# Pooled attention with a mixture-of-depths block: the first pair's queries copied by thirds, its keys all turned before the first scores

## The chip, the cores and the metric

The kernel runs on one core of a Trainium2 chip. A core has five engines that run their own instruction streams and wait for each other through semaphores: TensorE (matrix products and transposes; in the profile PE, its weight loads PEld), VectorE (DVE), ScalarE (ACT), GpSimd (POOL) and SyncE (SP), which here issues most transfers. The metric is the device time of one execution in microseconds. The kernel before takes 711.04 us, the median of three runs (710.81 to 711.89). Its profiled execution has a span of 707.8 us from the first to the last instruction, and all times inside a profile are counted from the start of that span.

## The reference

Two blocks follow one another. The first is attention whose queries are pooled by two along the sequence; the second routes 128 tokens of each batch entry through a small feed-forward network.

```python
# q, k, v: (8, 8, 1152, 64) float32
q_pool = q.reshape(B, H, S // 2, 2, D).mean(axis=3)          # 576 queries
scores = (1 / np.sqrt(D)) * np.matmul(q_pool, k.transpose(0, 1, 3, 2))
attn = np.exp(scores - scores.max(-1, keepdims=True))
attn = attn / (attn.sum(-1, keepdims=True) + 1e-09)
x = np.matmul(attn, v)                                       # then (B, 576, 512)
...
s = np.einsum('bsd,d->bs', x, w_gate)                        # a score per token
# the 128 best tokens of each batch entry b:
ye = np.maximum(xe @ w1, 0.0) @ w2                           # 512 -> 1024 -> 512
out[b, top_idx] = x[b, top_idx] + sigmoid(s)[:, None] * ye   # others: out = x
```

## The kernel before

Everything that the timed run does lies in the class `_Plain`; the other function in the file is a fallback for scores outside a numeric range. The work is cut into 32 **pairs** (8 batch entries times 4 pairs of heads), each pair into two **halves** of 288 of the 576 pooled queries. Keys and queries must stand with the head dimension on the partitions, "turned", before TensorE can multiply them: two heads of 64 fill the 128 partitions. `kT` holds the turned keys of a pair (128 x 1152), `qT` its turned and pooled queries (128 x 576).

For each half there are nine **blocks**, each of 128 keys (`scores`, L807). A block is four small products (quarter arrays, recorded as eight matmuls at L818) into one of four PSUM buffers, each two banks wide (`banks`, L996), and one exponential on ScalarE (L825) that moves the block to SBUF and so frees the buffer. GpSimd and VectorE sum the exponentials (`folded`, L859 and L864). The weighted sum with the values (`weighted`, L838) comes one half later. The order of all instructions on every engine is written out by hand in `run` (L1300): scores of half 0, scores of half 1, weighted sum of half 0, scores of half 2, weighted sum of half 1, and so on, with pieces of the routed feed-forward block (L1205, L1218) strewn in between. TensorE works through its instructions in that order. The framework adds the semaphore waits; it follows regions of a tile, so that a matmul waits only for the writers of the columns which it reads.

From the second pair on, keys and queries come in an order that lets VectorE turn them (L735, L739), in `prepare_pair`. **The first pair is special**, because nothing runs beside it. `load_first` (L741) fetches it in few, large pieces: queries on ScalarE's queue (L755), keys on SyncE's in four transfers (L759), first three of the nine chunks of both heads, then six of both; then the values (L762). `prepare_first` (L765) adds neighbouring queries (L776), and has TensorE turn keys (L783, in `keys`, L780) and queries (L794) against an identity matrix into PSUM. The results are copied to `kT` (L788) and `qT` (L801). The keys come in two steps: chunks 0 to 2 are turned first and copied by ScalarE; chunks 3 to 8 are turned later, by a function that `prepare_first` gives back. `run` hands it to the first call of `scores` as `behind_first`, where it is called once the first block and its exponential have been issued. VectorE copies that second part.

The six query transposes fill two PSUM banks, three transposes of 96 columns in each. A copy out of PSUM also has to sort columns: by their number's remainder by three (t in the code) they go into three thirds of `qT`, of 192 columns each. Before, VectorE copies bank 0 and ScalarE bank 1; each writes 96 columns in every third.

Ten products of ones (L612) run ahead of all this, while the data are on the way. `constants` (L616) follows `prepare_first` on VectorE and GpSimd: it makes tables that are used much later (slot numbers at L633, token numbers at L637, and so on).

Of the kernel before, what the change touches and what calls it, by code (L numbers as in the profile page):

```python
# [10 lines left out]
P = 128  # L11
BLK = 32

G = 3
# [13 lines left out]
def _any_scores(  # L28
# [451 lines left out]
    in_pair = [(j, t) for j in range(2) for t in range(NF)] + [(0, NF)]  # L480
    upcoming = load_pair(*pairs[0])
    run(prepare_pair(upcoming))
    preparing = iter(())
    routing = iter(())
# [50 lines left out]
class _Plain:  # L535
# [229 lines left out]
    def prepare_first(self, pair):  # L765

        nc, NC, D = self.nc, self.NC, self.D
        kT = pair["kT"] = self.load.tile([P, self.S], F32, name="kT")
        qT = pair["qT"] = self.load.tile([P, self.Sp], F32, name="qT")
        rows, third = 3 * BLK, self.QB // 3  # L770
        acc = self.work.tile([P, G, 2 * self.HALF], F32, name="acc")
        qp = acc.rearrange("p u n -> p (u n)")[0:rows, 0 : 2 * third * D]
        qp = qp.rearrange("p (n j d) -> p n j d", j=2, d=D)
        of = pair["q"].rearrange("p j (n r) d -> p n j r d", r=2)
        for j in range(2):
            nc.vector.tensor_tensor(  # L776
                out=qp[:, :, j, :], in0=of[:, :, j, 0, :], in1=of[:, :, j, 1, :], op=ALU.add
            )

        def keys(a, z, copy):  # L780
            ps = self.banks().rearrange("p b n -> p (b n)")
            for c in range(a, z):
                nc.tensor.transpose(  # L783
                    ps[:, (c - a) * P : (c - a + 1) * P],
                    pair["k"][:, c, :, :].rearrange("p j d -> p (j d)"),
                    self.ident[:, :],
                )
            copy(kT[:, a * P : z * P], ps[:, 0 : (z - a) * P])  # L788

        keys(0, G, nc.scalar.copy)  # L790
        ps = self.banks()
        per = third // 2
        for n in range(third):
            nc.tensor.transpose(  # L794
                ps[:, n // per, n % per * rows : (n % per + 1) * rows],
                qp[:, n, :, :].rearrange("p j d -> p (j d)"),
                self.ident[0:rows, 0:rows],
            )
        to = qT.rearrange("p (t b n i) -> p b n i t", t=3, b=2, i=BLK)
        for bank, copy in enumerate((nc.vector.tensor_copy, nc.scalar.copy)):  # L800
            copy(  # L801
                to[:, bank], ps[:, bank, 0 : per * rows].rearrange("p (n i t) -> p n i t", n=per, t=3)
            )

        return lambda: keys(G, NC, nc.vector.tensor_copy)

    def scores(self, half, behind_first=None):  # L807

        nc, pair, n = self.nc, half["pair"], self.HALF
        qs = slice(half["s"] * n, (half["s"] + 1) * n)  # L810
        p = half["p"] = self.work.tile([P, self.NG, G, 2, n], F32, name="p")
        for c in range(self.NC):
            sc = self.banks()
            for e in range(2):
                keys = slice(e * self.D, (e + 1) * self.D)
                for j in range(2):
                    rows = slice(j * self.D, (j + 1) * self.D)
                    nc.tensor.matmul(  # L818
                        sc[keys, j, 0:n],
                        lhsT=pair["kT"][rows, c * P + keys.start : c * P + keys.stop],  # L820
                        rhs=pair["qT"][rows, qs],
                        start=True,
                        stop=True,
                    )
            nc.scalar.activation(p[:, c // G, c % G, :, :], sc[:, :, 0:n], AF.Exp, scale=self.scale)  # L825
            if c == 0 and behind_first:
                behind_first()

    def weighted(self, half):

# [469 lines left out]
    def run(self):  # L1300
        nc = self.nc
        pairs = [(b, hp) for b in range(self.B) for hp in range(self.NPAIR)]
        n_halves = 2 * len(pairs)
        halves = []
        self.routing, self.waiting = [], set()
        upcoming = self.load_first(*pairs[0])
        self.first_constants()
        rest = self.prepare_first(upcoming)
        self.constants()
        loaded = self.load_pair(*pairs[1]) if len(pairs) > 1 else None  # L1310
        if loaded:
            self.load_values(loaded)
        self.load_gate()
        weights = self.weight_loads()
        for h in range(n_halves + 1):
            if h < n_halves:
                n, s = divmod(h, 2)
                if s == 0:
                    pair = upcoming
                    if pair["hp"] == 0:  # L1320
                        part = self.ffn.tile([P, self.NPAIR, self.QB], F32, name="part")
                    pair["part"] = part
                else:
                    loaded = None
                    if n + 2 < len(pairs):
                        loaded = self.load_pair(*pairs[n + 2])
                        self.load_values(loaded)
                    if n > 1:
                        self.stored(halves[h - 4]["pair"])
                if h > 1:  # L1330
                    next(weights, None)
                half = {"pair": pair, "s": s}
                halves.append(half)
                self.scores(half, rest if h == 0 else None)
                if h > 1:

                    of = halves[h - 2 - s]["pair"]
                    if s == 0:
                        of["groups"] = self.side_by_side(of["sum"].rearrange("p j n -> p (j n)"))
                    else:  # L1340
                        self.spread(of)
                if h > 2:
                    self.gated(halves[h - 3])
                self.folded(half)
                if h > 1:
                    self.multiplied(halves[h - 2])
                if s == 0 and loaded:
                    upcoming = loaded
                    self.prepare_pair(upcoming)
            else:  # L1350
                self.stored(halves[h - 3]["pair"])
                self.gated(halves[h - 3])
                self.multiplied(halves[h - 2])
                self.units()
            if h > 0:
                done = halves[h - 1]
                self.weighted(done)
                self.drained(done)
            if h == n_halves:
                self.multiplied(done)  # L1360
                self.gated(halves[h - 2])
            if 1 < h < n_halves and s == 0:
                done["pair"]["total"] = self.added(done["pair"]["groups"])
            if h == n_halves:
                self.normalized(done["pair"])
            elif h > 2 and s == 1:
                self.normalized(halves[h - 2]["pair"])
            if h < n_halves:
                self.units()
        for _ in weights:  # L1370
            pass

        self.stored(halves[-1]["pair"])


        self.gated(halves[-1])
        left = [unit for _, unit in self.routing]
        new = left.pop()
        old = left.pop() if left else iter(())
        older = left.pop() if left else iter(())  # L1380
        assert not left

        def pieces(unit, n=None):
            for i, _ in enumerate(unit):
                if i + 1 == n:
                    break

        pieces(older, self.NFC - 2)
        pieces(new, 1)
        pieces(older, 2)  # L1390
        pieces(new, 3)
        pieces(older)
        pieces(old, self.NFC)
        pieces(new, 1)
        low = self.counted()
        pieces(old, self.NFC - 3)
        pieces(new, 2)
        pieces(old)
        count = self.outside(low)
        pieces(new)  # L1400
        return nc.values_load(count[0:1, 0:1])
# [61 lines left out]
```

## Time and profile before

| what | value |
|---|---|
| device time, median of 3 | 711.04 us (710.81 to 711.89) |
| span of the profiled run | 707.8 us |
| TensorE busy | 696.5 us (98% of the span) |
| VectorE, ScalarE, GpSimd busy | 494.4, 443.3, 484.9 us |
| first score matmul (L818) begins | 8.87 us |
| exponentials (L825), mean of 576 | 690 ns |
| weighted sums of the first half (L838) begin | 18.98 us |

A line of a timeline gives the start, the duration, the engine, the line of the kernel, the operation, what it writes and reads with the shapes, and how many like it were merged; in square brackets stands how long the engine had been idle and what ended that. Consecutive instructions overlap in these records by a tenth of a microsecond or so[...]. The chain of work that ended last is found by walking back from the last instruction, at each step to whatever released it.

### The profile page before, as it was taken

The page shows a single profiled execution, that of the slowest core. Times are in us where ns is not written, and L with a number is a line of the kernel's source. Part 1 is how long each engine was busy: PE and PEld are TensorE (multiplying, and loading weights), DVE is VectorE, ACT ScalarE, POOL GpSimd, SP SyncE. Part 2 cuts the span into 40 slices and gives each one's busy share as a digit, 9 for nine tenths or more (in the row PEclk, how much of TensorE's full clock was granted, in tenths as well). Part 3 has the DMA queues.
Part 4 walks back from the last instruction along what each step waited for, and adds up shares of the span by engine and source line. Part 5 has one row for each costly group of instructions (what it writes and reads, how often), then busy time and mean ns, then how long its engine had stood idle before and what let it go on. Part 6 is the DMA issues. An engine that isn't in the chain of part 4 may idle for free.

```text
span 707.8 us, 23390 instructions
## 1 busy us (share of the span) xinstructions
PE 696.5 (98%) x9948; PEld 493.6 (70%) x9948; DVE 494.4 (70%) x793; ACT 443.3 (63%) x962; POOL 484.9 (69%) x452
## 2 busy tenths in 40 slices
PE   8999999999999999999999999999999999999996
PEld 6667887777857768576775777757776677767573
DVE  3877777896649965599654987549784597869540
ACT  5677777777547775477745777467754777577210
POOL 5777777877668685686955879557884777866520
PEclk9999999999999999999999999999999999999999
DMA  8888886849692385825967259662777428432200
GB/s 182 169 179 181 185 165 120 148 94 163 118 169 61 76 163 116 158 52 96 175 102 136 52 115 171 114 110 52 159 131 133 87 53 171 78 76 61 45 31 35
DMA packets 389490, 82.86 MB, mean 117 GB/s; under 512 B 376640, under 2 KB 376640, under 8 KB 389376
## 3 DMA queue, kind: packets, MB, share of 16 engines
q1 hardware_dynamic: 387872, 76.49, 57.2%
q0 software_dynamic: 1280, 4.20, 1.8%
q8 instruction: 80, 1.31, 0.8%
q10 hardware_dynamic: 224, 0.59, 0.3%
q14 instruction: 34, 0.28, 0.1%
HBM read 69.65 MB, written 11.59 MB: 115 GB/s over the span
## 4 chain that ended last, share of the span: by engine, by line
PE 95%; ACT 1%; POOL 1%; DVE 1%; DMA 1%; issue 0%; POOLq 0%; SPq 0%; DVEq 0%; ACTq 0%
PE ps L818 39%; PE ps L838 38%; PE ps L1205 8%; PE ps L1218 7%; ACT p L825 1%; DMA kb<-in_k_dram 1%; POOL acc L859 1%; PE ps L1194 1%; DVE fold L864 0%; POOL prod L927 0%; PE ps L783 0%; PE ps L1149 0%; ACT sums L904 0%; PE ps L1055 0%; POOL x L958 0%
## 5 line engine op out<-in xcount | busy, mean ns | idle before, releaser
L825 ACT ACTIVATE p<-ps 128x576 f32<-128x576 f32 x576 | 319.4, 690 | 3.3 <-PE ps L818 2.8
L859 POOL TENSOR_TENSOR acc<-p 128x576 f32<-128x576 f32 x192 | 266.1, 1415 | 54.3 <-ACT p L825 53.9
L818 PE MATMUL ps<-qT,kT 64*64 64x288 f32 x4608 | 296.2, 405 | 1.7 <-ACT qT L801 1.4
L838 PE MATMUL ps<-p,v_sb 64*64 64x288 f32 x4608 | 293.9, 403 | 0.0
L838 PEld LDWEIGHTS ps<-p,v_sb 64*64 64x64 f32 x4608 | 210.0, 133 | 71.1 <-ACT p L825 14.5
L818 PEld LDWEIGHTS ps<-qT,kT 64*64 64x64 f32 x4608 | 190.2, 133 | 94.4 <-ACT p L825 18.9
L864 DVE TRANSPOSE_TENSOR_REDUCE fold<-p 128x54 f32<-128x1728 f32 x64 | 126.0, 1969 | 118.5 <-ACT p L825 118.5
L864 DVE TRANSPOSE_TENSOR_REDUCE fold<-acc 128x54 f32<-128x1728 f32 x64 | 124.8, 1949 | 41.7 <-POOL acc L859 41.7
L846 ACT COPY two<-ps 128x576 f32<-128x576 f32 x64 | 40.9, 639 | 126.0 <-PE ps L838 113.2
L848 POOL TENSOR_TENSOR av<-two 128x288 f32<-128x288 f32 x64 | 51.2, 799 | 29.8 <-ACT two L846 28.2
L958 POOL TENSOR_TENSOR x<-avb,rec 128x576 f32<-128x576 f32 x32 | 37.0, 1157 | 43.1 <-DVE rec L956 26.4
L1205 PEld LDWEIGHTS ps<-xeT,w 128*128 128x128 f32 x512 | 57.8, 192 | 2.7 <-issue 2.6
L1205 PE MATMUL ps<-xeT,w 128*128 128x128 f32 x512 | 59.3, 277 | 0.0
L1218 PE MATMUL ps<-w,hT 128*128 128x512 f32 x128 | 57.3, 598 | 0.0
L927 POOL TENSOR_TENSOR prod<-avb,w_gate 128x288 f32<-128x288 f32 x64 | 51.4, 803 | 0.6 <-DVE avb L917 0.6
L904 ACT ACTIVATE sums<-total,tiny 32x18 f32<-32x18 f32 x124 | 38.2, 308 | 13.1 <-DVE total L895 11.4
L732 POOL TENSOR_TENSOR qp<-qb 128x576 f32<-128x576 f32 x31 | 43.8, 1413 | 0.9 <-DMA qb<-in_q_dram 0.9
L1218 PEld LDWEIGHTS ps<-w,hT 128*128 128x128 f32 x128 | 23.6, 190 | 28.1 <-issue 28.0
L735 DVE STREAM_TRANSPOSE kT<-kb 128x1152 f32<-128x1152 f32 x31 | 42.4, 1368 | 0.0
L1213 ACT ACTIVATE hT<-ps 128x512 f32<-128x512 f32 x16 | 9.6, 597 | 47.7 <-PE ps L1205 47.7
L1240 POOL TENSOR_TENSOR xe<-y,xe 128x512 f32<-128x512 f32 x7 | 8.9, 1270 | 38.4 <-ACT y L1237 38.4
L917 DVE STREAM_TRANSPOSE avb<-av 128x288 f32<-128x288 f32 x64 | 29.1, 455 | 7.2 <-POOL av L848 7.2
(95 smaller groups left out, 326.9 us busy)
## 6 DMA issues: line engine op xcount, KB each, us to landing
kb<-in_k_dram SPq DMA_DIRECT2D x124, 144.0 KB, 3.7
qb<-in_q_dram SPq DMA_DIRECT2D x124, 144.0 KB, 3.9
v_sb<-in_v_dram SPq DMA_DIRECT2D x124, 144.0 KB, 3.6
out_dram<-x SPq DMA_DIRECT2D x128, 72.0 KB, 3.0
lines<-row_rank SPq DMA_DIRECT2D x7, 640.0 KB, 4.2
w<-in_moe_w_dram SPq DMA_DIRECT2D x8, 512.0 KB, 5.0
sc_row<-row SPq DMA_DIRECT2D x7, 288.0 KB, 3.4
acc<-in_q_dram ACTq DMA_DIRECT2D x2, 288.0 KB, 4.2
```

What stands on the lines that cost most here:

```text
L732: nc.gpsimd.tensor_tensor(out=qp[:, :, :], in0=pair["q"][:, :, 0, :], in1=pair["q"][:, :, 1, :], op=ALU.add)
L735: nc.vector.transpose(kT.rearrange("p (c g i) -> p c g i", c=self.NC, i=BLK), pair["k"].rearrange("p (g c) d -> p c g d", c=self.NC),)
L818: nc.tensor.matmul(sc[keys, j, 0:n], lhsT=pair["kT"][rows, c * P + keys.start : c * P + keys.stop], rhs=pair["qT"][rows, qs], start=True, ...
L825: nc.scalar.activation(p[:, c // G, c % G, :, :], sc[:, :, 0:n], AF.Exp, scale=self.scale)
L838: nc.tensor.matmul(av[j * self.D : (j + 1) * self.D, e, 0:n], lhsT=half["pair"]["v"][keys, j, c, :], rhs=half["p"][keys, c // G, c % G, j, :],
L846: nc.scalar.copy(two[:, :, :], av[:, :, 0:n])
L848: nc.gpsimd.tensor_tensor(out=half["av"][:, :], in0=two[:, 0, :], in1=two[:, 1, :], op=ALU.add)
L859: nc.gpsimd.tensor_tensor(out=acc[:, u, :], in0=units[:, 0, u, :], in1=units[:, 1, u, :], op=ALU.add)
L864: nc.vector.tensor_reduce(fold[:, a, :], of.rearrange("p u (m d) -> p (u m) d", d=BLK), AX.X, ALU.add, apply_transpose=True,)
L927: self.nc.gpsimd.tensor_tensor(out=pair["prod"][:, ns, :], in0=pair["avb"][:, ns, :], in1=self.w_gate[:, hp : hp + 1, :].broadcast_to([P, ...
L1205: nc.tensor.matmul(pv[:, f, 0:w], lhsT=self.w1[:, c, (f0 + f) * P : (f0 + f + 1) * P], rhs=xeT[:, c, 0:w], start=(c == 0), stop=(c == self ...
L1218: nc.tensor.matmul(ps[0:w, 0 : self.Dm], lhsT=hT[:, f, 0:w], rhs=self.w2[:, f, :], start=(f == 0), stop=(f == self.NFC - 1),)
```

## The change

The change touches only the first pair. First, the transposes of key chunks 3 to 8 are issued to TensorE directly behind the query transposes, ahead of the first block of scores, and no longer between the first and second block. `keys` now issues transposes at once and gives back the copy, so that the copy can be placed apart: VectorE's copy of these chunks stands behind its query copy. Second, the query copies are cut by thirds of `qT` instead of by PSUM bank: VectorE takes the first 192 columns, ScalarE the second and the third 192, each with a read that steps by three and a write that is contiguous. The first half of the scores reads columns 0 to 287, so it needs the first two of the three copies. The hook `behind_first` in `scores` goes away. The aim is that TensorE and ScalarE run through the first blocks without a break, and that the query copies no longer write to interleaved places.

```diff
@@ in prepare_first
                     pair["k"][:, c, :, :].rearrange("p j d -> p (j d)"),
                     self.ident[:, :],
                 )
-            copy(kT[:, a * P : z * P], ps[:, 0 : (z - a) * P])
+            return lambda: copy(kT[:, a * P : z * P], ps[:, 0 : (z - a) * P])

-        keys(0, G, nc.scalar.copy)
+        keys(0, G, nc.scalar.copy)()
         ps = self.banks()
         per = third // 2
         for n in range(third):
...
-        to = qT.rearrange("p (t b n i) -> p b n i t", t=3, b=2, i=BLK)
-        for bank, copy in enumerate((nc.vector.tensor_copy, nc.scalar.copy)):
-            copy(
-                to[:, bank], ps[:, bank, 0 : per * rows].rearrange("p (n i t) -> p n i t", n=per, t=3)
-            )
-
-        return lambda: keys(G, NC, nc.vector.tensor_copy)
+        copy_keys = keys(G, NC, nc.vector.tensor_copy)
+        to = qT.rearrange("p (t b n i) -> p t b n i", t=3, b=2, i=BLK)
+        of = ps[:, :, 0 : per * rows].rearrange("p b (n i t) -> p t b n i", n=per, t=3)
+        copies = (nc.vector.tensor_copy, nc.scalar.copy, nc.scalar.copy)
+        for t, copy in enumerate(copies):
+            copy(to[:, t], of[:, t])
+        copy_keys()

@@ in scores
             nc.scalar.activation(p[:, c // G, c % G, :, :], sc[:, :, 0:n], AF.Exp, scale=self.scale)
-            if c == 0 and behind_first:
-                behind_first()

@@ in run
-        rest = self.prepare_first(upcoming)
+        self.prepare_first(upcoming)
...
-                self.scores(half, rest if h == 0 else None)
+                self.scores(half)
```

More of the change, by code (lines that the diff above doesn't have):

```diff
@@ L798, in prepare_first, with scores @@
             )
-        to = qT.rearrange("p (t b n i) -> p b n i t", t=3, b=2, i=BLK)
-        for bank, copy in enumerate((nc.vector.tensor_copy, nc.scalar.copy)):
-            copy(
-                to[:, bank], ps[:, bank, 0 : per * rows].rearrange("p (n i t) -> p n i t", n=per, t=3)
-            )
-        return lambda: keys(G, NC, nc.vector.tensor_copy)
-    def scores(self, half, behind_first=None):
+        copy_keys = keys(G, NC, nc.vector.tensor_copy)
[5 more added lines that the diff above has]
+        copy_keys()
+    def scores(self, half):
         nc, pair, n = self.nc, half["pair"], self.HALF
```

## The prediction

> **What bounds the kernel now.** I began with the page: busy shares first, then the chain of work that ended last.
>
> ```profile
> PE 696.5 (98%) x9948; PEld 493.6 (70%) x9948; DVE 494.4 (70%) x793; ACT 443.3 (63%) x962; POOL 484.9 (69%) x452
> ...
> PE 95%; ACT 1%; POOL 1%; DVE 1%; DMA 1%; issue 0%; POOLq 0%; SPq 0%; DVEq 0%; ACTq 0%
> ```
>
> TensorE carries 95% of the chain. Every matmul of the steady state stays as it is, so the change can only be worth what the start is worth. Next I read the chain over the first 30 us (start, length, what):
>
> ```profile
> 1.29 4.85 DMA kb<-in_k_dram
> 6.14 0.14 issue
> 6.28 0.65 PE ps L783 x3
> 6.93 0.51 PE ps L794 x6
> 7.44 0.02 issue
> 7.46 0.66 DVE qT L801
> 8.12 0.02 issue
> 8.14 0.68 ACT qT L801
> 8.82 0.04 issue
> 8.87 0.71 PE ps L818 x8
> 9.58 0.81 PE ps L783 x6
> 10.39 1.13 PE ps L818 x16
> ```
>
> Key DMA, three key transposes, six query transposes, two query copies **one after the other**, the first score block, then six more key transposes that split that block from the second. After it the chain is solid PE. Third, ScalarE's timeline there, and what TensorE's weighted sums waited for:
>
> ```profile
> 9.65 0.65 ACT L825 ACTIVATE p<-ps 128x576 f32<-128x576 f32 x1 [0.84 <-PE ps L818]
> 11.10 5.11 ACT L825 ACTIVATE p<-ps 128x576 f32<-128x576 f32 x9 [0.80 <-PE ps L818]
> ```
> ```profile
> 18.15 0.78 ACT L825 ACTIVATE p<-ps 128x576 f32<-128x576 f32 x1
> ```
> ```profile
> 18.98 0.21 PEld L838 LDWEIGHTS ps<-p,v_sb 64*64 64x64 f32 x8 [0.34 <-ACT p L825]
> ```
>
> This is the reading that matters. Two halves of scores (18 blocks, 18 exponentials) run before the first weighted sum. A block costs TensorE 4.37/9 = 0.486 us (the chain has 4.37 for 72 matmuls, nine blocks). ScalarE starts an exponential every 0.53 us: from 11.10 to 18.15 there are 13 starts, 7.05 us, of which 0.12 is one wait for the late keys. So in this stretch **ScalarE sets the pace**: four PSUM buffers are all it lets TensorE run ahead, and the weighted sums begin at 18.98, when the 15th exponential (18.15 + 0.78 = 18.93) frees their buffer. What moves that 15th exponential moves the rest. ScalarE lost its time between its first exponential (9.65) and its second (11.10): 1.45 us where back to back takes 0.55.
>
> [...] The old copies read one bank each; the new ones, by thirds, each read both[...]. The trace of before does not show such a pair: its ScalarE copy also waited for the VectorE one (0.70 us idle), but there the banks were different and the destinations interleave in qT. [...] 288 columns took 0.648 and 0.668 us[...]; these write with a long stride. [...] the key transposes at 9.51 lie between two score blocks. So moving them ahead of the first scores makes these wait for the second key DMAs too.
>
> **The change, part by part.**
>
> *Transposes moved ahead.* Their keys are the third and fourth key DMAs. The fourth is issued at 2.35 and its landing is listed as 5.4 us later: 7.75. The query transposes end at 7.43. From landing to transpose took 0.14 after the first key DMAs, so the six start at about 7.87. At 9.51 they held TensorE 0.80 (first transpose to first matmul after them, 10.32)[...]. The scores could then start at 7.87 + 0.85 = **8.72**, not 8.87. Behind the wait in TensorE's queue are only the scores; they need the queries anyway.
>
> *Three query copies.* Not in the trace. [...] From above, no cheaper than the old 288: 0.65 and 0.67. I take the old ones scaled in their columns with 0.16 fixed (ScalarE's 384 and 576 columns, 0.479 and 0.639, give 0.83 ns a column and 0.16): 0.16 + (2/3) x 0.49 = 0.49 on VectorE and 0.50 on ScalarE. The first half of the scores reads columns 0 to 287, so it needs the first third (VectorE) and the second (first on ScalarE). One after the other from 7.46: 7.46 + 0.49 + 0.03 + 0.50 = 8.48, scores 0.06 later at 8.54. [...]from above 8.87. At my value the keys are later by 0.18, so the copies **cost nothing here**; at the upper end they set the start and it stays at 8.87. ScalarE's other third runs to about 9.0, behind the key wait and the first scores, before the first exponential wants the engine at 9.50; and its PSUM buffer is next written by the third block, after 9.6.
>
> *The wait between the first and second block goes.* This is the larger part. New: first exponential 0.78 after the start of the scores (9.65 - 8.87), the second 0.55 later, 13 more at 0.53: the 15th starts at start + 0.78 + 0.55 + 6.89 = start + 8.22. Before: 18.15 - 8.87 = start + 9.28. **1.06 saved**, with the small wait at the fourth block inside it.
>
> *Copy of the late keys (VectorE, 0.96).* It waits for the transposes, about 8.8 to 9.76. The fourth block, the first that reads these keys, comes at 8.72 + 3 x 0.49 = 10.2. Hidden. Behind it VectorE's constants move from 7.96 to about 9.8-10.7. GpSimd's small add at L660 waits for one of them, and its first sum of exponentials stands behind that: wanted at about 11.8, free by 10.5. Nothing.
>
> *Sum:* (8.87 - 8.72) + 1.06 = **1.2 us**.
>
> *Does it reach the end?* The second pair's load doesn't move: its query sum on GpSimd runs at 17.50 behind a DMA, and ends at 18.91. VectorE then turns the queries, before at 21.12 to 21.87; the folds ahead of it come 1.2 earlier, so about 20.65. TensorE wants these 1.2 earlier than 23.4, at 22.2. Slack 1.5. The next pair's turned queries end at 35.37 by the same reading and are wanted at about 41. Beyond this the chain is TensorE, and the tail after 646 us hangs on TensorE's last scores. I let all of it through: 711.04 - 1.2 = **709.85**.
>
> **Rivals.**
> *More (18%).* The second keys land earlier in the timed runs[...]. Without a wait for the DMA the six transposes follow the queries at 7.26, and 0.85 later the scores could come, at 8.1[...]. For it: the key DMAs land only 0.3 behind the query transposes. Against it: in this profile they do land behind, with the 16 DMA engines busy.
> *Little or nothing (13%).* Later keys: a landing 0.9 later leaves 0.3. Or what is gained at 19 us is eaten by GpSimd's first two sums of exponentials, the second of which (18.87) does not move because it stands behind the second pair's query sum. For it: those second sums (18.87 to 23.02) would then end 0.5 after VectorE wants them (21.78 + 1.96 - 1.2 = 22.5). Against it: VectorE and GpSimd are 70% busy and have 2.9 and 1.4 us idle in the very next half. 710.6.
> *Slower (7%).* Everything behind one gate: a key landing after 9.5. Before, the first block was done by then; after, it still has to come, and pays one exponential more, 0.55. 711.6. In favour, only that the scores now wait for four key DMAs instead of two. Against: 9.5 would be 1.75 us after the landing seen.
>
> **How the numbers follow.** Forecast 62%, the rivals 18, 13 and 7. 0.2% is 1.42 us, so the forecast's 1.2 counts as no change, as does the little-or-nothing case. Over 1.42 faster: nearly all of the first rival and a sixth of the forecast's spread (copy times, landing, scatter of a measurement, whose three runs cover 1.1 us): 0.28. Over 1.42 slower: part of the last, 0.05. The range goes from the first rival's gain with a little scatter, 709.1, to just past little-or-nothing, 710.8; outside it stay the slower case and the edges of the others.
>
> **What would show it.** Right: the nine key transposes (L783) and six query transposes in one run, with a gap before the last six of about 0.4 ended by the key DMA; first score matmul at 8.6 to 8.8; exponentials with no gap from 9.5 on; weighted sums from about 17.75 instead of 18.98; the span shorter by the same. The step on the copies is wrong if the first score matmul waits for ScalarE's copy; the one on the gate if the keys are there before 7.4; the one on the carry if TensorE waits in its third half of scores, at 22 to 27 us, for turned queries or for exponentials. The prediction fails upward if the landing of the fourth key DMA varies much from run to run, as everything now hangs on it.

## The result, and the profile after

The changed kernel takes 708.18 us, the median of six runs (707.89 to 709.5). The kernel before, timed beside it, takes 710.79 (709.41 to 711.89). The ratio is 0.997, with an interval at 95% of 0.9956 to 0.9985: 1 to 3 us less. The forecast was 709.85 with a range of 709.1 to 710.8, so the time lies **below the range**. The direction was right; of the 2.6 us between the medians about half was not foreseen.

The page of the changed kernel first: the busy line, and the shares of the chain that ended last.

```profile
PE 695.8 (99%) x9948; PEld 499.9 (71%) x9948; DVE 494.4 (70%) x793; ACT 442.8 (63%) x963; POOL 484.9 (69%) x452
...
PE 92%; POOL 3%; issue 1%; DVE 1%; DMA 1%; ACT 1%; SPq 0%; POOLq 0%; DVEq 0%; ACTq 0%
```

TensorE still carries the chain; one instruction more stands on ScalarE (963 instead of 962: the third query copy). The chain over the first 25 us (start, length, what):

```profile
2.34 5.51 DMA kb<-in_k_dram
7.86 0.14 issue
7.99 0.84 PE ps L783 x6
8.84 9.20 PE ps L818 x144
18.03 4.42 PE ps L836 x72
```

Behind the key DMA only three pieces of TensorE work are left up to 22.5 us. The last keys land at 7.86, 0.14 later their transposes run, then all 18 blocks of scores follow in one piece (x144), then the first half's weighted sums. The timeline of TensorE, VectorE and ScalarE there shows the same from the engines' side:

```profile
6.77 0.66 PE L794 MATMUL ps<-ident,acc 96*128 96x96 f32 x6
7.47 0.36 DVE L804 COPY qT<-ps 128x192 f32<-128x192 f32 x1 [0.91 <-PE ps L794]
7.86 0.54 ACT L804 COPY qT<-ps 128x192 f32<-128x192 f32 x2 [0.41 <-DVE qT L804]
7.99 0.84 PE L783 MATMUL ps<-ident,kb 128*128 128x128 f32 x6 [0.56 <-DMA kb<-in_k_dram]
8.77 9.26 PE L818 MATMUL ps<-qT,kT 64*64 64x288 f32 x144
8.88 0.96 DVE L788 COPY kT<-ps 128x768 f32<-128x768 f32 x1 [1.05 <-PE ps L783]
9.55 9.89 ACT L825 ACTIVATE p<-ps 128x576 f32<-128x576 f32 x18 [1.16 <-PE ps L818]
```

All 18 exponentials stand in one line with no idle time inside: the gap between the first and the second (9.65 to 11.10 before) is gone. The start of the weighted sums, from the weight loads:

```profile
17.86 0.21 PEld L836 LDWEIGHTS ps<-p,v_sb 64*64 64x64 f32 x8 [0.34 <-ACT p L825]
```

That is 1.12 us earlier than 18.98, and the forecast was 1.2. So this trace confirms the whole start and explains 1.1 of a difference of 2.6 us. The two profiled executions differ by 1.67 us (709.66 before, 707.99 after); the other half microsecond lies in places where the two have the same instructions: 0.2 at about 112 us and 0.24 behind TensorE's last matmul. The 0.2 is no chance: at that place 0.79 us pass from the start of ScalarE's copy to that of its next exponential in all six profiled kernels that copy the queries by bank, and 0.54 in all eight that copy them by thirds. What links the two is not known. The larger remainder is in neither trace: **the profiled execution of the kernel before took 709.66 us, less than each of its first three timed ones** (710.81 and up).

### The profile page after: what moved, and what is told of

Read it like the earlier page. It is cut to its first block, busy times and chain, and to the rows that moved or that the text cites. A ratio compares the mean times of both kernels' runs of the same rounds, so it can differ in the third digit from the quotient of the medians.

```text
span 706.3 us, 23391 instructions
## 1 busy us (share of the span) xinstructions
PE 695.8 (99%) x9948; PEld 499.9 (71%) x9948; DVE 494.4 (70%) x793; ACT 442.8 (63%) x963; POOL 484.9 (69%) x452
## 3 DMA queue, kind: packets, MB, share of 16 engines
q8 instruction: 80, 1.31, 0.8%
## 4 chain that ended last, share of the span: by engine, by line
PE 92%; POOL 3%; issue 1%; DVE 1%; DMA 1%; ACT 1%; SPq 0%; POOLq 0%; DVEq 0%; ACTq 0%
PE ps L818 38%; PE ps L836 37%; PE ps L1203 8%; PE ps L1216 7%; POOL acc L857 2%; DMA kb<-in_k_dram 1%; PE ps L1192 1%; POOL prod L925 0%; ACT p L825 0%; POOL x L956 0%; DVE fold L862 0%; POOL av L846 0%; SPq L759 0%; PE ps L1147 0%; PE ps L1053 0%
## 5 line engine op out<-in xcount | busy, mean ns | idle before, releaser
L836 PEld LDWEIGHTS ps<-p,v_sb 64*64 64x64 f32 x4608 | 213.2, 133 | 67.8 <-ACT p L825 14.3
L818 PEld LDWEIGHTS ps<-qT,kT 64*64 64x64 f32 x4608 | 193.3, 132 | 89.8 <-ACT p L825 18.5
```

The lines of the kernel that those rows point to most:

```text
L818: nc.tensor.matmul(sc[keys, j, 0:n], lhsT=pair["kT"][rows, c * P + keys.start : c * P + keys.stop], rhs=pair["qT"][rows, qs], start=True, ...
L836: nc.tensor.matmul(av[j * self.D : (j + 1) * self.D, e, 0:n], lhsT=half["pair"]["v"][keys, j, c, :], rhs=half["p"][keys, c // G, c % G, j, :],
```

## The experiments

The question is where the second half of the gain comes from. The theories: *order*, called A in the expectations (only what the forecast counts, and the rest is scatter); B (a second gain of about 1 us later in the program); *copies* (the thirds bring something by themselves); and *clock*, called C, formed from the scatter and then from the profiles: the kernel before often loses TensorE's clock in the idle stretches of its start, and the changed kernel rarely does. The **granted clock** is the share of TensorE's full clock that the profile records; the **mean clock** of an execution is its mean over the whole span. Each kernel was timed in five rounds, in three sets; those of a set ran beside the same runs of the kernel before, whose medians were 713.26 us (40 runs), 710.79 (27 runs) and 713.12 (61 runs). Times are compared within a set, except where the text says otherwise.

### First set: which part does it, and how steady is the kernel before?

**The changed kernel again** (no edit) and **the kernel before against itself** (no edit).

> The changed kernel once more, to measure it finer. Theory A (the start alone): the weighted sums of the first half begin at 17.8 to 17.9 us instead of 18.98, and nothing else is gained; beside the kernel before on the same chip it is 1.1 to 1.4 us faster, a ratio of about 0.998. Theory B (a second gain, later in the program, of about 1 us): 2.0 to 2.6 us faster, a ratio of 0.9965 or so, and the shift between the two traces grows again somewhere after 20 us in this profile too.

> The kernel before against itself: the ratio is 1.000, and its interval shows what scatter between executions there is. Theory A, by which part of the measured 2.6 us is scatter, expects single times that lie 1 us or more apart, with spans that differ by as much although the first 20 us agree within 0.2 us. Theory B expects a scatter well below 1 us. In the profile the wait of 0.15 us before an exponential at 112.66 should be gone, or stand elsewhere, if it was chance.

The changed kernel: 710.22 us, ratio 0.9963 (0.995 to 0.9976). The gain is there again, at 2 to 3 us. The kernel before: 712.27, ratio to itself 0.9985 (0.9972 to 0.9997), with single times from 710.61 to 714.06. Two times of one kernel lie up to 3.5 us apart, and the 14 runs of it have a median 1.0 us under that of the other 40. So the intervals are somewhat too narrow, and **a difference of up to 1 us between two medians shows nothing here**. B falls: from the first weighted sums to TensorE's last matmul the changed kernel needs 683.9 us in this profile and the kernel before 683.6, so nothing is gained there. Nor is the short wait at 112 us chance, since it is there again (at 115 us). The profiled execution of the kernel before happened to be a long one, with a span of 712.1 us against 707.8, and its first 20 us do not agree with those of the first profile, although A expects that they do. Its TensorE, in stretches of 3.41 us (stretch, length, busy time and instructions, granted clock, DMA share, GB/s):

```profile
5.04:8.45 3.41, 1.62 (x12) 1.00 1.19 286
8.45:11.86 3.41, 2.79 (x18) 0.50 1.01 160
11.86:15.28 3.42, 3.42 (x32) 0.50 0.93 146
15.28:18.69 3.41, 3.41 (x64) 1.00 0.95 217
```

The cuts are those of the trace's own record of the clock. TensorE is busy for 1.62 of 3.41 us, and then **runs at half its clock for 6.83 us**. What that does to the first blocks is seen on TensorE and ScalarE:

```profile
9.07 1.24 PE L818 MATMUL ps<-qT,kT 64*64 64x288 f32 x8 [1.44 <-ACT qT L801]
10.23 1.54 PE L783 MATMUL ps<-ident,kb 128*128 128x128 f32 x6
```
```profile
10.37 0.65 ACT L825 ACTIVATE p<-ps 128x576 f32<-128x576 f32 x1 [1.35 <-PE ps L818]
13.01 0.65 ACT L825 ACTIVATE p<-ps 128x576 f32<-128x576 f32 x1 [1.99 <-PE ps L818]
13.97 0.65 ACT L825 ACTIVATE p<-ps 128x576 f32<-128x576 f32 x1 [0.31 <-PE ps L818]
```

The first block takes 1.24 us instead of 0.71 and the six transposes 1.54 instead of 0.87. ScalarE, which sets the pace at full clock, has to wait 1.99 for the second block and 0.31 for the next ones. The weighted sums begin at 21.82 instead of 18.98: 2.8 us lost that the profile before does not show. Such a return to half the clock during the start is called a **fall** below.

**Only the transposes ahead** (the old copies by banks stay):

```diff
-        to = qT.rearrange("p (t b n i) -> p t b n i", t=3, b=2, i=BLK)
-        of = ps[:, :, 0 : per * rows].rearrange("p b (n i t) -> p t b n i", n=per, t=3)
-        copies = (nc.vector.tensor_copy, nc.scalar.copy, nc.scalar.copy)
-        for t, copy in enumerate(copies):
-            copy(to[:, t], of[:, t])
+        to = qT.rearrange("p (t b n i) -> p b n i t", t=3, b=2, i=BLK)
+        for bank, copy in enumerate((nc.vector.tensor_copy, nc.scalar.copy)):
+            copy(
+                to[:, bank], ps[:, bank, 0 : per * rows].rearrange("p (n i t) -> p n i t", n=per, t=3)
+            )
         copy_keys()
```

> Only the transposes ahead; the queries are still copied by PSUM bank, VectorE then ScalarE. By my reading this is nearly the whole change: the copies end at 8.81, so the first scores start at 8.87 instead of 8.77, the exponentials run without a gap from 9.65, the weighted sums begin at about 17.95, and the kernel is 1.0 us faster than before (ratio 0.9985). The rival, that the copies by thirds carry the gain, expects no more than 0.3 us here.

710.39 us, ratio 0.9962 (0.9948 to 0.9976), the same as the whole change. ScalarE's longer copy now holds the scores up by 0.15:

```profile
8.93 9.26 PE L818 MATMUL ps<-qT,kT 64*64 64x288 f32 x144 [0.15 <-ACT qT L802]
9.71 9.89 ACT L825 ACTIVATE p<-ps 128x576 f32<-128x576 f32 x18 [0.84 <-PE ps L818]
```

**Only the thirds** (in the kernel before; its transposes still split the first two blocks):

```diff
-        to = qT.rearrange("p (t b n i) -> p b n i t", t=3, b=2, i=BLK)
-        for bank, copy in enumerate((nc.vector.tensor_copy, nc.scalar.copy)):
-            copy(
-                to[:, bank], ps[:, bank, 0 : per * rows].rearrange("p (n i t) -> p n i t", n=per, t=3)
-            )
+        to = qT.rearrange("p (t b n i) -> p t b n i", t=3, b=2, i=BLK)
+        of = ps[:, :, 0 : per * rows].rearrange("p b (n i t) -> p t b n i", n=per, t=3)
+        copies = (nc.vector.tensor_copy, nc.scalar.copy, nc.scalar.copy)
+        for t, copy in enumerate(copies):
+            copy(to[:, t], of[:, t])
```

> Only the copies by thirds; the late key transposes still stand between the first and second block. The copies measured 0.36 and 0.32 us in the changed kernel, so the second ends at 8.18 and the first scores start at about 8.23 instead of 8.87. The late keys have landed (7.86) when their transposes come, so everything moves by 0.64, and the gap of 0.8 us between the first two exponentials stays: weighted sums at 18.35, 0.6 us faster than before (ratio 0.999). The rival, that ScalarE's pace and not the start of the scores decides, and the first gap hides all, expects nothing.

711.32 us, ratio 0.9981 (0.997 to 0.9993). The scores begin at 8.47 and the weighted sums at 18.58, 0.4 earlier than before (8.23 and 18.35 were expected); its gap between the exponentials stays:

```profile
8.47 0.72 PE L818 MATMUL ps<-qT,kT 64*64 64x288 f32 x8 [0.80 <-ACT qT L803]
```
```profile
9.25 0.65 ACT L825 ACTIVATE p<-ps 128x576 f32<-128x576 f32 x1 [0.61 <-PE ps L818]
10.70 9.46 ACT L825 ACTIVATE p<-ps 128x576 f32<-128x576 f32 x17 [0.80 <-PE ps L818]
```

The two parts do not add up: the early transposes alone bring everything, and the thirds alone bring less. By its times this kernel can't even be told from the kernel before, whose ratio to itself is 0.9985. Behind the early transposes the thirds save a wait of 0.15 us at the start of the trace and the 0.2 at about 112 us, and nothing that the times can show (710.22 against 710.39). The copies theory falls. The idle time of TensorE ahead of the scores is 0.8 us in this kernel and 1.44 in the kernel before, which is why the clock theory also expects something of it.

### Second set: is it the clock?

**The kernel before, with its gap filled.** Five products of ones, which nothing reads, stand behind the query transposes, where TensorE idles 1.44 us. The order is otherwise the old one.

```diff
+        busy = self.banks()[:, 0, 0:P]
+        for _ in range(5):
+            nc.tensor.matmul(busy, lhsT=self.ones[:, :], rhs=self.ones[:, :], start=True, stop=True)
```

> The kernel before, with five products of ones ([...]their result is not used) put between the query transposes and the first scores, where TensorE stands idle for 1.44 us. They delay nothing while the clock is full. Theory C (in some executions of the kernel before, TensorE's clock goes to half near 8.5 us because of that idle time, as one profile of it showed, and the start then takes some 2.8 us longer): the long executions go, the median falls by 1 to 2.5 us against before, the shortest times stay where they are, and the clock record has no half-speed stretch before the tail. Rival (the order of the work alone): no change, or slower by up to 0.2 us.

710.27 us, ratio 0.9989 (0.9979 to 0.9999). Half of this expectation came true. The falls of the clock are gone: its 13 executions have a mean clock of 0.997 or more, while 16 of the 27 of the kernel before are at 0.995 or less. But the time went down by 0.5 us only, which is less than the kernel before differs from itself. Its profile shows how the products can be in the way:

```profile
6.97 1.17 PE L794 MATMUL ps<-ident,acc 96*128 96x96 f32 x6
7.93 2.33 PE L801 MATMUL ps<-ones 128*128 128x128 f32 x10
10.18 0.71 PE L821 MATMUL ps<-qT,kT 64*64 64x288 f32 x8
```

In this execution TensorE had not yet reached its full clock (the trace's record begins at 10.05, where it does; before, it began at 6.57). The query transposes took 1.17 us instead of 0.66, the five products 2.33 instead of the 1.31 that they take at full clock (in the profile of the last experiment), and the scores waited for them. So there is a **second kind of loss, a late rise**, and here the filler makes it dearer. The mean clock does not tell it (0.998 for this execution): it counts only what the record holds, and the record starts with the first rise in this profile (10.05), in the one before (6.57) and in one of the third set (10.48).

The single times of the kernel before in this set show both losses. Its 27 executions stand in three groups: eight from 709.19 to 709.9 us, all with a mean clock of 0.997 or more; ten from 710.51 to 711.2, all at 0.995; nine from 711.79 to 712.38, six of them at 0.994 or less and three at 0.997 or more, which fits a late rise. The first group has a median of 709.4, the whole set one of 710.79.

**The changed kernel with a late gate.** The values are issued between the second and the third key DMA, so that the last keys land later.

```diff
         for a, z in ((0, G), (G, NC)):
+            if a:
+                for j, h in enumerate(heads):
+                    of = self.v[b, h].rearrange("(p c) d -> p c d", c=NC)
+                    nc.sync.dma_start(v_sb[:, j, :, :], of)
             for j, h in enumerate(heads):
                 of = self.k[b, h].rearrange("(p c) d -> p c d", c=NC)
                 nc.sync.dma_start(kn[:, a:z, j, :], of[:, a:z, :])
-        for j, h in enumerate(heads):
-            of = self.v[b, h].rearrange("(p c) d -> p c d", c=NC)
-            nc.sync.dma_start(v_sb[:, j, :, :], of)
```

> The changed kernel with its second pair of key transfers issued behind the values instead of ahead of them. The gate of the prediction (the fourth key transfer): it lands at about 9.4 instead of 7.86, so the six transposes start at 9.5 and the scores at 10.35 instead of 8.77: 1.6 us slower than the changed kernel, 0.4 slower than the kernel before when nothing disturbs either. Theory C adds: TensorE is idle for 2.1 us ahead of the transposes, so that the clock goes to half in many executions; times spread over 3 us as those of the kernel before do, and the median is 2.5 us or more above that of the changed kernel. Without C: 1.6 us, and a spread of about 1 us.

711.97 us, ratio 1.0018 (1.0007 to 1.0029): 1.2 us above the kernel before. TensorE's timeline and its stretches:

```profile
9.61 0.85 PE L784 MATMUL ps<-ident,kb 128*128 128x128 f32 x6 [2.31 <-DMA kb<-in_k_dram]
10.38 10.72 PE L819 MATMUL ps<-qT,kT 64*64 64x288 f32 x144
20.93 3.38 PE L837 MATMUL ps<-p,v_sb 64*64 64x288 f32 x52
```
```profile
4.30:7.71 3.41, 1.80 (x16) 1.00 1.10 302
7.71:11.13 3.42, 1.52 (x18) 1.00 1.09 167
11.13:14.54 3.41, 3.41 (x32) 0.50 0.90 142
```

The scores begin at 10.38, 1.6 us later than in the changed kernel. By the gate alone that would cost 1.6. It costs 3.9 against the changed kernel with its gap filled, in the same set (708.05, below). The longer idle stretch (2.31 us) also takes the clock: 11 of its 14 executions have a mean clock of 0.996 or less. The profiled execution (711.11 us) shows what that does: its weighted sums come 3.07 later than in the changed kernel's profile, twice what the gate accounts for. This is the clock theory seen from the other side: a longer wait in the *changed* order brings the kernel-before's trouble back, and more often.

**Keys that need no wait.** The keys are stored head by head, so that they arrive in pieces of 768 and 1536 bytes, not 256; TensorE then turns them one head at a time by products with the identity.

```diff
-        kn = kb.rearrange("p n d -> p (n d)").rearrange("p (c j d) -> p c j d", c=NC, j=2)
+        kn = kb.rearrange("p n d -> p (n d)").rearrange("p (j c d) -> p c j d", c=NC, j=2)
...
-                nc.tensor.transpose(
-                    ps[:, (c - a) * P : (c - a + 1) * P],
-                    pair["k"][:, c, :, :].rearrange("p j d -> p (j d)"),
-                    self.ident[:, :],
-                )
+                for j in range(2):
+                    nc.tensor.matmul(
+                        ps[j * D : (j + 1) * D, (c - a) * P : (c - a + 1) * P],
+                        lhsT=pair["k"][:, c, j, :],
+                        rhs=self.ident[:, :],
+                        start=True,
+                        stop=True,
+                    )
```

> The changed kernel with the first pair's keys kept head by head in SBUF, so that a transfer's contiguous pieces are 768 and 1536 bytes instead of 256, and turned by products with the identity for each head (64 columns each) instead of by transposes of both heads. If the landing of the keys is the gate and larger pieces land sooner: fourth key transfer at 6.9 to 7.4 instead of 7.86, scores at 8.25 to 8.6 instead of 8.77, up to 0.5 us faster than the changed kernel. If the doubled number of products costs as much as that: no difference.

708.27 us, ratio 0.9959 (0.9946 to 0.9972), no better than the changed kernel with its gap filled (708.05, below). The keys do come earlier, and no wait is left:

```profile
7.47 1.53 PE L784 MATMUL ps<-ident,kb 128*64 128x128 f32 x24
8.94 3.38 PE L821 MATMUL ps<-qT,kT 64*64 64x288 f32 x52
```

The transposes begin right behind the queries, at 7.47 instead of 7.99, but twice as many of them take 1.53 us instead of 0.84, and the scores begin at 8.94, not 8.77. TensorE's longer work ate what the DMA gave.

**The changed kernel with its gap filled** by two products of ones (as above, with `range(2)`).

> The changed kernel with two products of ones in its remaining idle stretch of 0.56 us ahead of the late key transposes. Theory C says that 0.56 us is not enough to lose the clock, so: the same as the changed kernel within 0.2 us, and the same spread. If a rest of clock loss is still in the changed kernel: 0.3 to 0.5 us faster in the median.

708.05 us, ratio 0.9962 (0.9947 to 0.9977). The changed kernel as it is was not run in this set; beside a kernel before of the same median (710.79) it had 708.18 in the first result. So there is no sign of a clock loss in the changed kernel that the filler could mend.

### Third set: the two losses apart

Ten products of ones run at the very start. Two more would lengthen the busy stretch, against the late rise; the filler of the second set is against the fall. Here both are used together and apart, in the two kernels:

```diff
-        for _ in range(10):
+        for _ in range(12):
             nc.tensor.matmul(ps, lhsT=self.ones[:, :], rhs=self.ones[:, :], start=True, stop=True)
```

The changed kernel once more, without an edit, to stand beside these:

> The changed kernel, so that it stands in one set with the three below. Theory C (the change is worth 1.1 to 1.2 us by the order of its start, and the rest because TensorE's clock no longer falls to half): its undisturbed executions lie 1.2 us under the shortest of the kernel before, at about 708.0 if these are at 709.2, its median 2 to 2.7 us under the median of before. The order alone: 1.2 us in the median as well.

710.18 us, ratio 0.9966 (0.9954 to 0.9978). The changed kernel with twelve ones and two products in its gap:

> The changed kernel with 12 instead of 10 products of ones ahead of everything, and two more in the stretch of 0.56 us before the late key transposes[...]. Theory C: median as the changed kernel's within 0.2 us, without single executions 1 us or more above it.

710.34 us, ratio 0.9966 (0.9955 to 0.9977). The longest execution is shorter (711.36 against 712.0, though still 1.0 above the median), the median does not move. So no version found here beats the change itself. The kernel before with twelve ones:

> The kernel before with 12 instead of 10 products of ones ahead of everything, the idle 1.44 us left as they are. By theory C two things make the kernel before long: the clock that falls again in the idle stretch, and, in one execution of six or so, a clock that rises late (near 10 us or later instead of 4 to 7)[...]. This removes the second alone: executions around 2.5 us above the shortest whose clock record shows no fall should go, those with a fall stay; median up to 0.5 us under before. The order alone: no change.

711.75 us, ratio 0.9982 (0.9972 to 0.9992), further under the kernel before than the 0.5 us that were expected. Six of its 22 executions still have a mean clock of 0.996 or less. But the long executions without a fall are gone: of the 61 of the kernel before, 12 lie over 713 us at a mean clock of 0.997 or more, and here there is none. That fits a late rise which the two added products prevent. The kernel before with twelve ones and the five products:

> The kernel before with 12 products of ones ahead and five in the idle 1.44 us: [...]the order of the work stays as before. Theory C: all executions within 0.5 us of the shortest of the kernel before (about 709.3 if that is 709.2), so 1.2 us above the changed kernel, which is then the worth of the order, and 1.3 to 1.6 us under the median of before, which is the worth of the clock. The order alone: same median as before.

711.86 us, ratio 0.9987 (0.9977 to 0.9996). The expectation that all its executions lie within 0.5 us of the shortest of the kernel before (710.35) failed: they go from 710.45 to 712.74. Nor is the median under that of the twelve ones alone. But all its 22 executions have a mean clock of 0.997 or more, none lies over 713 us, and its start is that of the undisturbed profile before: the scores begin at 8.92 and the weighted sums at 19.03 (8.87 and 18.98 there).

```profile
8.92 0.71 PE L821 MATMUL ps<-qT,kT 64*64 64x288 f32 x8 [0.31 <-ACT qT L804]
...
19.03 1.20 PE L841 MATMUL ps<-p,v_sb 64*64 64x288 f32 x16
```

As far as the mean clock and this profile tell, this kernel is the old order without the clock's trouble, and so it gives an **estimate of the split**: 713.12 - 711.86 = 1.3 us is what the kernel before loses to the clock at the median, and 711.86 - 710.34 = 1.5 what the change is worth without that. By its interval it lies 0.3 to 1.6 us under the kernel before, and the kernel before differed from itself by 1.0 in the first set, so this run alone does not show the clock's part. The groups of the second set say the same more clearly: 710.79 - 709.4 = 1.4 us for the clock, and 709.4 - 708.05 = 1.35 for the rest. The traces give 1.1 at the start and 0.2 at 112 us. The shortest executions of this set, 710.35 for the kernel before and 709.3 for the changed one, are 1.05 apart.

The two kinds of loss can still be seen in this set. With twelve ones alone one profile has a fall:

```profile
5.94:9.36 3.42, 1.62 (x15) 1.00 1.21 279
9.36:12.77 3.41, 3.41 (x22) 0.50 0.88 138
```

and the changed kernel's profile has a late rise (the record begins at 10.48, and the column shows 1.00 where there is no record yet):

```profile
3.65:7.07 3.42, 2.66 (x13) 1.00 1.23 268
7.07:10.48 3.41, 3.41 (x22) 1.00 1.00 234
```

Its scores begin at 9.48 and its weighted sums at 19.05, 1.2 later than in the first profile after. The change does not cure that kind.

## Why the prediction was wrong, and where it was right

**Right: the scores.** Forecast at 8.72, found at 8.77. The landing was put at 7.75 and came at 7.86. The gap ahead of the last six transposes is 0.56, ended by the key DMA, as the prediction asked (about 0.4). The forecast's 0.85 from the first of them to the scores was the 0.80 of the trace and 0.05 of my own estimate; found was 0.78 (7.99 to 8.77).

**Too dear, without effect: the query copies.** I took 0.49 and 0.50 us, scaled from the old ones. They took 0.36 on VectorE and 0.32 to 0.33 on ScalarE. With the forecast's fixed 0.16 taken off, that is 1.0 and 0.8 ns a column (192 columns), where the old copies have 1.7 and 1.8 (0.648 and 0.668 us for 288). What sets the old ones apart is a write that jumps from third to third of `qT`, 192 columns on, at each element. That this is the reason was not tested by itself. The new ones did follow one another: ScalarE's waited 0.41 for VectorE's. As forecast, they cost nothing, since the keys gate the scores.

**Right: the gap between the exponentials.** 1.06 forecast. The 15th exponential moved from 18.15 to 16.99, that is 1.16, of which 0.10 is the earlier start of the scores: 1.06.

**Right: the late keys' copy is hidden**, from 8.88 to 9.84 (forecast 8.8 to 9.76), and the constants behind it cost nothing.

**Right: it carries to the end.** VectorE turned the second pair's queries at 20.01 to 20.74, 1.1 earlier than before (the forecast for the end was 20.65), with no new wait in TensorE. VectorE did wait 0.27 for GpSimd's second sum of exponentials (at 22.87), as the rival of little or nothing has it; TensorE did not feel it. Between the shortest executions of the two kernels lie 1.52 us in the first result, 1.31 in the first set and 1.05 in the third.

**Of the rivals**, "more" came nearest (its scores at 8.1 give 8.87 - 8.1 + 1.06 = 1.8 us, that is 709.2), with the wrong cause: in the profile the keys did not land earlier, and where they did (the packed keys) nothing was gained. "Slower" had the right mechanism: late keys (transposed from 9.61 on) make the kernel slower than before. It left out the clock: the median is 1.2 us above the kernel before, where it says 0.6, and 3.9 above the changed kernel, where the gate alone accounts for 1.6.

**The step that failed is the last: "I let all of it through: 711.04 - 1.2 = 709.85."** The 1.2 was worked out from the one profiled execution, in which TensorE kept its full clock (mean 0.999). The 711.04 is a median of three executions that by their times did not: the six of the first result (709.41 and 709.51; 710.77, 710.81 and 711.04; 711.89) fall into the same three groups as those of the second set, and the three of the forecast's median are in the two groups that lost clock. (Their own mean clocks are not on record.) From the profiled execution's own time the same sum gives 709.66 - 1.2 = 708.46, which is 0.3 from the result. The term left out is what the old order loses to the clock, about 1.4 us at the median. I read the 1.1 us between the three runs as scatter of a measurement, and charged TensorE's idle 1.44 us with its own length only.

To see how often the clock falls, I counted the timed executions with a mean clock of 0.996 or less. The count is rough, since the mean also holds a stretch at half clock at the very end, behind the last matmul: in the profile before from 706.30 us on, in the one after from 705.09 on. The profile of the changed kernel again has a mean of 0.997 without a fall in its start. Of the profiles, the three with 0.996 or less (the kernel before again, late keys, and twelve ones in the old order) show a fall at the start, and the others show none.

| kernel | executions | at 0.996 or less |
|---|---|---|
| before, three sets and against itself | 142 | 72 |
| before, gap filled (two kernels) | 35 | 0 |
| the change, unedited (first result, sets 1 and 3) | 31 | 3 |
| the change with late keys | 14 | 11 |

In the second and third set the kernel before has a median of 709.52 and 711.8 above that mark and of 710.89 and 713.4 at or below it, so 1.4 to 1.6 us lie between the two. In the first set the difference is 0.3 only, since there 12 of the 22 executions above the mark are over 713 us as well; by what the profiles show these had a late rise, though that was not seen in their own traces.

Why the order can help the clock, too: before, TensorE stood idle for 0.60 and 1.44 us on both sides of a short piece of work. After, it idles 0.83 and 0.56. The first of the two changes with the landing of the keys (0.92 in the kernel before again, 1.61 in the changed kernel again); what the change takes away is the 1.44. These are the stretches, cut to the record's own grid, in the profile before:

```profile
3.15:6.57 3.42, 2.82 (x14) 1.00 1.19 267
6.57:9.98 3.41, 1.97 (x21) 1.00 1.09 257
```

and after:

```profile
5.35:8.77 3.42, 2.02 (x18) 1.00 1.20 282
8.77:12.18 3.41, 3.41 (x57) 1.00 0.97 148
```

In these two executions each kernel has one stretch that is just over half busy, and keeps the clock. The grid does not start with the kernel (cuts at 6.57 here, at 5.04 and 5.94 in other executions of the old order), and so it seems to be a matter of luck whether both of the old kernel's gaps fall into one stretch.

**Left open.** In the profiles of sets 1 and 3 both orders need 1.5 to 2.2 us more from the first weighted sums to TensorE's last matmuls than in the first result and in set 2; no cause was found, which is why times are compared within a set. The split of the gain, 1.1 to 1.5 for the order and the rest for the clock, is an estimate. Fillers take the falls away, but the medians fall by 0.5 and 1.3 us only, so that the clock's part was never removed cleanly. That a fall and a late rise come about by the phase of the grid is inferred from the profiles shown; the phase was not set by any experiment.

## What to carry to other kernels

Before a saving read from one profile is taken off a median, compare the profiled execution's own time and mean clock with the timed ones; if it is faster than all of them, the profile may not show what the typical execution loses. A short start-up gap on TensorE can cost more than its length, since it can take the clock from the work behind it (here a gap of 1.44 us stood ahead of a start that took 2.8 us longer); filling it with unread products took the falls from 72 of 142 executions to 0 of 35 here, but only helps if these products are not themselves in the way. When work is moved ahead of a wait, take the idle time that the move closes between pieces of TensorE work into the sum.

## What the runs showed of the hardware

The granted clock of TensorE is either 1.0 or 0.5 in the stretches shown here, and the times at which it changes fit a grid of 3.41 us. In the profiles before and after it is 1.0 from 6.57 to 706.30 us and from 5.35 to 705.09, both times for 699.73 us. In the kernel before again it falls at 8.45 and rises at 15.28, 6.83 us later; with twelve ones it falls at 9.36 and rises at 12.77, 3.41 us later.

No idle stretch in the start of the kernel before is longer than 1.5 us (1.44 in its profiles), and it still loses the clock. What tells the stretches apart is their busy share: the clock fell after 45% (late keys, 1.52 of 3.42 us) and 47% (1.62 us, twice, in the old order), and was kept after 53% (1.80), 58% (1.97) and 59% (2.02). So in these traces a stretch that lost the clock was at most 47% busy, and one that kept it at least 53%.

The rises came after fuller stretches: after one that was 82% busy (2.79 us, in the kernel before again) the clock stayed at half, and after 78% (2.66, the changed kernel in the third set) the first rise did not come, though after another of 82% (2.82, in the profile before) it did. After the seven fully busy stretches at half clock (3.41 or 3.42 us, in five profiles) it came each time. So the fall with full work behind it lasted 3.41 us (twelve ones, late keys), and the other one 6.83.
